# Two groups of a layer's matmuls moved up between the steps of a retention chain

## The chip, the core and the metric

One core of one Trainium2 chip runs the whole program in one launch. The metric is device time in microseconds. The kernel before takes 770.5 us as the median of three runs (770.07 to 770.96). TensorE is called PE here (PEld is its weight load), VectorE is DVE, ScalarE is ACT, GpSimd is POOL, and SP issues the DMAs.

## The reference

Three stages follow each other. Retention (linear attention with a decay per head) makes x; a gated layer without activation multiplies two products of x; a second layer has a leaky activation with a slope for each channel.

```python
batch, n_heads, seq, head_dim = (4, 8, 576, 64)
scores = scale * np.matmul(q, k.transpose(0, 1, 3, 2))
gamma = 1.0 - 2.0 ** (-5.0 - np.arange(H))
Dmat = np.where(rel >= 0, gamma[:, None, None] ** rel[None, :, :], 0.0)
x = np.matmul(scores * Dmat, v)              # then (2304 tokens, 512)
a = x @ w1; b = x @ w2                       # 512 -> 1024
x = (a * b @ w3) @ w_out                     # 1024 -> 1024 -> 512
h = x @ w_in                                 # 512 -> 2048
g = np.maximum(h, 0.0) + alpha * np.minimum(h, 0.0)
out = g @ w_out2                             # 2048 -> 512
```

## The kernel before

**Retention.** The sequence of a batch b is cut into five pieces c (four of 128 tokens, one of 64), and the pieces are taken one after the other, since each carries a state to the next. For batches 1 to 3 this is a chain of 15 links (`chain`, L721); link i treats piece i = 5(b-1)+c. In `link` (L723) PE issues three things: `scores` of the *next* piece (L406, L395 for the short one; PSUM tile `sc`), `values` of this piece (L448 from the state, L457 from the masked scores; tile `o`) and `moments` of the next piece (L421; tile `st`). Everything that other engines do with these results is put on a list, `later`, and issued when the next link begins (`flush`): DVE multiplies `sc` by the mask (L410, L398), and PE's L457 waits for that product; ACT copies `o` into x (L469); DVE adds `st` to the state (L429), and POOL ages it (L433). The pool of `sc` has two buffers (L675), so the scores of piece i+1 may be written while DVE still reads those of piece i. Eight PSUM banks are in use: one for warm-up matmuls, four for `sc`, two for `o`, one for `st`.

**Work beside the links.** The table `beside` (L759) says which preparations for the next stage are issued after which link: `ready` scales q and k of a coming batch (POOL L383, L385; pair 3 on DVE), `ab_steps` prepares the weights' operands, and `x_steps(n)` issues the next n of nine steps that make x's operands of a token pair of blocks p (`x_operands`, L628). A step holds an ACT cast (L637), a DVE subtraction for the low half (L641) and sometimes a DVE difference (L645), each on 128x768.

**First layer.** Its products run in 24 groups of seven (`AbGroup`, L815: p1, p5, p6, p2, p7, p3, p4; a Strassen-like scheme with seven products for eight). A product is six matmuls of 128x384 (L807). The group has three PSUM banks b1, b2, b3; ACT copies b1 to b2 (L830), and b3, b2, b1 to SBUF (L834, L838, L842); DVE makes the two factors from them and multiplies (L847, L852, L859, L860). A finished group is written to DRAM (`spill`). The first three groups begin with a dummy matmul (L827). The groups stand in `ab_order` (L938), n = 0 is weight chunk 0 with p = 0, n = 1 chunk 1 with p = 0, then chunks 0 and 1 with p = 1 and p = 2, then chunk 2 (n = 6 to 8) and so on. Preparations that go beside group n are in `todo`, filled by `at(n, "a" | "b" | "c", ...)` (L950). From n about 5 on this holds the pieces of the folded weights too (`ws_tick`), whose third step is a copy on ACT (L128) of what DVE made (L122).

**Order.** PE, ACT and SP run in the order of the code in the whole kernel; DVE and POOL do so until the end of retention (`ordered`, L690 to L783). After that a list scheduler orders DVE's instructions.

Of the kernel before, what the change touches and what calls it, by code (L numbers as in the profile page):

```python
# [7 lines left out]
F32 = mybir.dt.float32  # L8
# [152 lines left out]
def retention_moe_kernel(ctx: ExitStack, tc, qk, kv, w_out1, w3t, w12, w_in, w_out2, alpha, c_row, c_pair, out):  # L161
# [49 lines left out]
    def kib(flat, at, n):  # L211
        return flat[:, 256 * at:256 * at + n]
# [149 lines left out]
    class Retention:  # L362
# [24 lines left out]
        def scores(self, c):  # L387
            b, n = self.b, self.n
            sc = self.psum["sc"].tile([P, 2, 512], F32, tag="sc", name=f"sc{b}_{c}")
# [278 lines left out]
    def some_of(steps, n):  # L668
        for _ in range(min(n, len(steps))):
            steps.pop(0)()  # L670


    first = ExitStack()
# [76 lines left out]
    def x_steps(n):  # L750
        return lambda: some_of(make, n)

    def to_xr():
# [10 lines left out]
        3: [ready(rs[2], 2), ready(rs[2], 3, nc.vector), x_steps(1)],  # L764
        4: [lambda: load_batch(3), ab_steps(1, "f1"), x_steps(1)],
        5: [x_steps(1), ab_steps(1, "s1")],
        6: [ready(rs[3], 0), x_steps(2)],
        7: [ready(rs[3], 1), x_steps(1), ab_steps(1, "h0")],
        8: [ready(rs[3], 2), ready(rs[3], 3, nc.vector), ab_steps(1, "l0")],
        9: [x_steps(2), ab_steps(1, "h1")],  # L770
        10: [to_xr, lambda: make.extend(ab_operands(1)), ab_steps(1, "l1 h2"), x_steps(1)],
        11: [ab_steps(1, "l2"), x_steps(1)],
        12: [x_steps(1)],
        13: [x_steps(1)],
        14: [x_steps(2)],
    }
    for i in range(-1, len(chain)):
        link(i)()
        for run in beside.get(i, ()):
            run()  # L780
    flush()
    flush()
    ordered.close()  # L783
# [9 lines left out]

    class Group:


        def __init__(self, p, j, n):
            self.p, self.j, self.n = p, j, n
            self.b1, self.b2, self.b3 = (bank((3 * n + m) % 8, f"h{n}_{m}")[:, :W] for m in range(3))

        def product(self, ps, a, b, fresh=True):
            a, b = self.operand(self.j, a), xop[self.p, b]
            n = 0
            for k in range(2):
                ks = slice(k * P, (k + 1) * P)
                for x, y in ((0, 0), (0, 1), (1, 0)):
                    nc.tensor.matmul(ps, a[:, x, ks], b[:, y, k], start=(fresh and n == 0), stop=(n == 5),  # L807
                                     skip_group_check=True)
                    n += 1

    abd = [scratch.tile([P, C1, 2, W], F32, tag=f"ab{p}", name=f"abd{p}") for p in range(NP)]
    fives = [kib(xs, 0, 2 * W)[:, W * m:W * m + W] for m in range(2)]
    pairs_of = [kib(xs, 3 + 3 * m, 2 * W).rearrange("p (t n) -> p t n", t=2) for m in range(3)]

    class AbGroup(Group):  # L815


        operand = staticmethod(ab_operand)

        def __init__(self, p, j, n):  # L820
            super().__init__(p, j, n)
            self.p5s, self.f = fives[n % 2], pairs_of[n % 3]

        def p1(self):
            if self.n < 3:

                nc.tensor.matmul(self.b2, self.operand(self.j, "A11")[:, 0, 0:P], xop[self.p, "B11"][:, 0, 0],  # L827
                                 start=True, stop=True)
            self.product(self.b1, "A11", "B11")
            nc.scalar.copy(self.b2, self.b1)  # L830

        def p5(self):
            self.product(self.b3, "S1", "T1")
            nc.scalar.copy(self.p5s, self.b3)  # L834

        def p6(self):
            self.product(self.b2, "S2", "T2", False)
            nc.scalar.copy(self.f[:, 1], self.b2)  # L838

        def p2(self):  # L840
            self.product(self.b1, "A12", "B21", False)
            nc.scalar.copy(self.f[:, 0], self.b1)  # L842

        def p7(self):
            self.product(self.b2, "S3", "T3", False)
            with soon():
                nc.vector.tensor_tensor(out=self.p5s, in0=self.b2, in1=self.p5s, op=ALU.add)  # L847

        def p4(self):
            self.product(self.b2, "A22", "T4", False)  # L850
            with soon():
                nc.vector.tensor_tensor(out=self.f[:, 0], in0=self.b2, in1=self.f[:, 0], op=ALU.mult)  # L852
            later.append(self.spill)

        def p3(self):
            self.product(self.b3, "S4", "B22", False)
            u = self.f[:, 1]
            with soon():
# [833 lines left out]
```

## Time and profile before

| what | value |
|---|---|
| median of three runs | 770.5 us (770.07 to 770.96) |
| the profiled execution: its own time | 770.14 us |
| its span in the trace | 768.4 us |
| PE busy | 746.7 us (97%) |
| DVE busy | 640.2 us (83%) |
| ACT busy | 428.4 us (56%) |
| POOL busy | 30.2 us (4%) |
| mean granted TensorE clock | 0.991 of full speed |
| last link ends, first layer begins | 88.23 us |

The profile is of one execution, whose own time lies 1.7 us above its span. Busy time of PE counts matmuls by modelled ends, so overlapping ones and those at half the clock count in full; PEld, the weight loads, keeps closer to the pace at which matmuls can be issued. "Idle before" in square brackets behind a row is the engine's idle time just before it, and the arrow names what ended it.

### The profile page before, as it was taken

Reading aid. Unit: us, or ns where it says so; the run is one execution under the profiler, and the core shown is the slowest. Engines: PE = TensorE matmul, PEld = TensorE weight load, DVE = VectorE, ACT = ScalarE, POOL = GpSimd, SP = SyncE. Lnnn points to the kernel's source line nnn. Section 1 sums busy time; section 2 is a strip of 40 time slices with the busy share of each in tenths; the row PEclk is TensorE's granted clock in tenths of the full one; section 3 lists DMA queues with packets and bytes.
Section 4 is the critical chain, followed back from the end, with each engine's and each line's share of the span. In section 5 each row is a group of like instructions: output and inputs, shape, how many; then the busy total and the mean of one; then the engine's idle time right before and its main releaser. Section 6 shows DMA issues by size and latency. Waiting matters only on the chain.

```text
span 768.4 us, 13325 instructions
## 1 busy us (share of the span) xinstructions
PE 746.7 (97%) x4979; PEld 698.3 (91%) x4979; DVE 640.2 (83%) x1061; ACT 428.4 (56%) x754; POOL 30.2 (4%) x35
## 2 busy tenths in 40 slices
PE   8887899999999999999999999999999999999998
PEld 4676899999999988999999999999999888888887
DVE  4899987999799869999997879979877777877884
ACT  3565466666476546666765557556545444444442
POOL 1345000000000000000000000000000000000000
PEclk9899999999999999999999999999999999999999
DMA  9963135676547986587764997666999754434430
GB/s 337 387 249 148 58 123 174 223 242 220 204 170 248 370 315 219 199 308 258 285 225 158 323 369 273 238 208 230 323 351 404 219 158 131 130 120 142 132 122 28
DMA packets 106848, 173.25 MB, mean 225 GB/s; under 512 B 8096, under 2 KB 73888, under 8 KB 106784
## 3 DMA queue, kind: packets, MB, share of 16 engines
q1 hardware_dynamic: 106784, 172.40, 64.7%
q8 instruction: 39, 0.64, 0.3%
q14 instruction: 25, 0.20, 0.1%
HBM read 112.34 MB, written 60.03 MB: 224 GB/s over the span
## 4 chain that ended last, share of the span: by engine, by line
PE 80%; DVE 11%; DMA 5%; issue 2%; ACT 1%; SPq 1%; DVEq 0%; ACTq 0%
PE h L807 37%; PE o L1403 15%; PE y L1219 13%; PE o L1405 8%; PE pw L1059 6%; DMA xs<-in_kv_dram 2%; DMA raw<-in_w_dram 1%; DMA heads_r<-in_kv_dram 1%; DVE wa L641 1%; DVE heads_l L410 1%; PE o L457 1%; DVE xs L645 1%; DVE wa L568 0%; DMA xs<-in_w3t_dram 0%; PE st L421 0%
## 5 line engine op out<-in xcount | busy, mean ns | idle before, releaser
L1219 PE MATMUL y<-yab,wa 128*128 128x384 f32 x576 | 100.2, 334 | 0.0
L1219 PEld LDWEIGHTS y<-yab,wa 128*128 128x128 f32 x576 | 99.8, 188 | 0.3 <-DVE yab L1041 0.2
L1384 DVE TENSOR_TENSOR cells<-cells,cells 128x1024 fp32r<-128x1024 f32 x63 | 76.3, 1220 | 23.3 <-ACT cells L1378 23.3
L1403 PE MATMUL o<-wa,cells 128*128 128x512 f32 x288 | 76.6, 393 | 0.0
L1378 ACT CAST cells<-cells 128x1024 fp32r<-128x1024 f32 x63 | 64.9, 1054 | 5.8 <-DVE cells L1371 5.1
L1403 PEld LDWEIGHTS o<-wa,cells 128*128 128x128 f32 x288 | 51.4, 189 | 8.5
L807 PE MATMUL h<-xB,wa 128*128 128x384 f32 x288 | 58.0, 335 | 0.1
L1403 PE MATMUL o<-wop,cells 128*128 128x512 f32 x216 | 56.9, 392 | 0.0
L807 PE MATMUL h<-xl,wa 128*128 128x384 f32 x288 | 56.2, 336 | 0.6 <-ACT h L830 0.6
L807 PE MATMUL h<-xT,wa 128*128 128x384 f32 x288 | 56.5, 334 | 0.0
L807 PEld LDWEIGHTS h<-xl,wa 128*128 128x128 f32 x288 | 50.2, 188 | 1.9 <-ACT h L830 1.9
L807 PE MATMUL h<-wa 128*128 128x384 f32 x264 | 51.4, 335 | 0.0
L807 PEld LDWEIGHTS h<-xB,wa 128*128 128x128 f32 x288 | 50.5, 188 | 0.6 <-DVE xB L641 0.6
L807 PEld LDWEIGHTS h<-xT,wa 128*128 128x128 f32 x288 | 50.5, 188 | 0.0
L807 PE MATMUL h<-xr,wa 128*128 128x384 f32 x240 | 47.0, 335 | 1.3 <-ACT h L830 0.7
L1403 PEld LDWEIGHTS o<-wop,cells 128*128 128x128 f32 x216 | 39.4, 188 | 7.7
L807 PEld LDWEIGHTS h<-wa 128*128 128x128 f32 x264 | 46.2, 188 | 0.2 <-ACT h L830 0.2
L1405 PEld LDWEIGHTS o<-wa,cells 128*128 128x128 f32 x288 | 41.8, 190 | 3.5
L1405 PE MATMUL o<-wa,cells 128*128 128x256 f32 x288 | 44.5, 282 | 0.0
L807 PEld LDWEIGHTS h<-xr,wa 128*128 128x128 f32 x240 | 41.9, 188 | 1.9 <-ACT h L830 1.0
L1275 DVE SCALAR_TENSOR_TENSOR g<-h,al,g 128x384 f32<-128x384 f32 x48 | 29.1, 612 | 12.1 <-ACT g L1273 10.1
L122 DVE CUSTOM_DVE_ANT_0 a<-a,b 128x1024 uint16<-128x1024 uint16 x56 | 38.3, 685 | 0.5
(238 smaller groups left out, 1535.1 us busy)
## 6 DMA issues: line engine op xcount, KB each, us to landing
gd<-g SPq DMA_DIRECT2D x96, 192.0 KB, 4.5
cells<-gd SPq DMA_DIRECT2D x36, 512.0 KB, 6.0
abd<-xs SPq DMA_DIRECT2D x24, 384.0 KB, 3.2
yf<-abd SPq DMA_DIRECT2D x24, 384.0 KB, 6.2
rawi<-in_w_in_dram SPq DMA_DIRECT2D x16, 512.0 KB, 6.0
wod<-wo2u SPq DMA_DIRECT2D x28, 256.0 KB, 2.6
wa<-wod SPq DMA_DIRECT2D x12, 512.0 KB, 7.0
wod<-xs SPq DMA_DIRECT2D x21, 256.0 KB, 3.1
```

Of the source, the lines that this page charges most:

```text
L122: nc.vector.tensor_tensor(out=a.bitcast(I32), in0=a.bitcast(I32), in1=b, op=ALU.add)
L410: later.append(lambda: nc.vector.tensor_tensor(out=rt, in0=sc[:, :, 0:n * CH].rearrange("p h (n i) -> p h n i", n=n), in1=mask[:, :, self.ps],
L457: nc.tensor.matmul(o[pp, p % 2, m // 2, 0:w], vj, rj, start=(c == 0 and m < 2), stop=True, skip_group_check=True)
L641: nc.vector.tensor_tensor(out=t[:, 1], in0=src[op], in1=_f32(t[:, 0]), op=ALU.subtract)
L807: nc.tensor.matmul(ps, a[:, x, ks], b[:, y, k], start=(fresh and n == 0), stop=(n == 5), skip_group_check=True)
L1059: nc.tensor.matmul(acc[i], a[:, ic], bb, start=(k == 0 and n == 0), stop=(k == C1 - 1 and n == 2))
L1219: nc.tensor.matmul(ys[o], wpc[c][a][:, oc], yab[u][:, bb, c % 2], start=(c == 0 and i == 0), stop=(c == C1 - 1 and i == 2))
L1275: nc.vector.scalar_tensor_tensor(out=g, in0=ps, scalar=sal[:, c], in1=g, op0=ALU.mult, op1=ALU.max)
L1378: nc.scalar.copy(h.bitcast(F32R), self.q[name])
L1384: nc.vector.tensor_tensor(out=l.bitcast(F32R), in0=q[name], in1=h, op=ALU.subtract)
L1403: nc.tensor.matmul(ps, h[:, k], w[k], start=(fresh and k == 0), stop=(k == C1 - 1), skip_group_check=True)
L1405: nc.tensor.matmul(ps[:, 256:], l[:, k], w[k][:, 0:256], start=False, stop=(k == C1 - 1), skip_group_check=True)
```

## The change

The groups n = 0 and n = 1 leave the loop of the layer and are issued inside the chain, a product at a time: one after link 7 has begun, two in each of links 8 to 13 and one in link 14 (`FILLS`). The first product of a link stands ahead of its `scores`, the second behind its `moments`, and what DVE and ACT do with the second one's result goes on `later`. Three PSUM banks are needed for this; they come from the warm-up bank and from the second buffer of `sc`, so from batch 2 on (link 4's `scores`) `sc` has one buffer. The two groups keep their SBUF results in the space of x's block pair 0. The table of x's operands is dealt out anew: block pair 0's nine steps now stand in links 2, 5, 6, 7 and 8 (before: 2 to 7 and 9), block pair 1's first seven in links 10 to 14 (before six), and the rest, with block pair 2's and weight chunk 2's, beside groups 2 to 6 (before: 0 to 6). The class `Group` and `AbGroup` moved up in the file; their unchanged lines are left out here.

```diff
-        return flat[:, 256 * at:256 * at + n]
+        return flat[:, int(256 * at):int(256 * at) + n]
...
         def scores(self, c):
             b, n = self.b, self.n
-            sc = self.psum["sc"].tile([P, 2, 512], F32, tag="sc", name=f"sc{b}_{c}")
+            self.psum["sc"].reverse()
+            sc = (self.psum["sc"][0] if b < 2 else self.psum["late"]).tile([P, 2, 512], F32, tag="sc", name=f"sc{b}_{c}")
...
-        def __init__(self, p, j, n):
+        def __init__(self, p, j, n, banks=None):
             self.p, self.j, self.n = p, j, n
-            self.b1, self.b2, self.b3 = (bank((3 * n + m) % 8, f"h{n}_{m}")[:, :W] for m in range(3))
+            banks = banks or [bank((3 * n + m) % 8, f"h{n}_{m}") for m in range(3)]
+            self.b1, self.b2, self.b3 = (x[:, :W] for x in banks)
+            self.then = lambda run: run()
...
+    EARLY = 2
+    early_of = [(kib(xs, a, W), kib(xs, f, 2 * W).rearrange("p (t n) -> p t n", t=2))
+                for a, f in ((4, 9), (5.5, 0))]
...
-            self.p5s, self.f = fives[n % 2], pairs_of[n % 3]
+            self.p5s, self.f = (fives[n % 2], pairs_of[n % 3]) if n >= EARLY else early_of[n]
...
-            if self.n < 3:
+            if self.n == 0 or EARLY <= self.n < EARLY + 3:
...
             self.product(self.b1, "A11", "B11")
-            nc.scalar.copy(self.b2, self.b1)
+            self.then(lambda: nc.scalar.copy(self.b2, self.b1))
...
-    warm = pool(first, "ps_warm", space=PSUM).tile([P, 512], F32, name="warm")
-    psum0 = {"sc": pool(first, "ps_sc", bufs=2, space=PSUM, reuse_waits="tile"),
+    psum0 = {"late": pool(first, "ps_sc", space=PSUM, reuse_waits="tile"),
...
+    early = ExitStack()
+    warm = pool(early, "ps_warm", space=PSUM).tile([P, 512], F32, name="warm")
+    psum0["sc"] = [psum0["late"], pool(early, "ps_sc1", space=PSUM, reuse_waits="tile")]
...
+    FILLS, fill = {7: 1, 8: 2, 9: 2, 10: 2, 11: 2, 12: 2, 13: 2, 14: 1}, []
+
+    def early_groups():
+        pe = pool(first, "ps_early", space=PSUM, reuse_waits="tile")
+        banks = [pe.tile([P, 512], F32, tag=f"e{m}", name=f"e{m}") for m in range(3)]
+        groups = [AbGroup(0, c, c, banks) for c in range(EARLY)]
+        return [(g, step) for g in groups for step in (g.p1, g.p5, g.p6, g.p2, g.p7, g.p3, g.p4)]
+
     def link(i):
         def run():
             flush()
             nxt = chain[i + 1] if i + 1 < len(chain) else None
+            if i == min(FILLS):
+                early.close()
+                fill.extend(early_groups())
+            n = FILLS.get(i, 0)
+            if n:
+                g, step = fill.pop(0)
+                step()
             if nxt:
                 rs[nxt[0]].scores(nxt[1])
...
                 rs[nxt[0]].moments(nxt[1])
+            if n == 2:
+                g, step = fill.pop(0)
+                g.then = later.append
+                step()
+                g.then = lambda run: run()
...
-        3: [ready(rs[2], 2), ready(rs[2], 3, nc.vector), x_steps(1)],
+        3: [ready(rs[2], 2), ready(rs[2], 3, nc.vector)],
...
-        6: [ready(rs[3], 0), x_steps(2)],
+        6: [ready(rs[3], 0), x_steps(2), ab_steps(1, "s1")],
...
+    abu.load(6)
     ordered.close()
...
-    at(0, "a", x_steps(1))
...
-    at(1, "c", x_steps(2), ab_steps(2, "f0"))
...
+    at(2, "a", x_steps(2), make_p2)
...
+    at(2, "c", x_steps(1), ab_steps(2, "f0"))
+    at(3, "a", x_steps(1), ab_steps(2, "s0 f1"))
+    at(3, "b", x_steps(2))
...
     for n, (c, p) in enumerate(ab_order):
+        if n < EARLY:
+            continue
```

The instructions as they stand in the built programs show what this makes of the queues. First PE in links 7 and 8, before (`sc2_3` are the scores of batch 2's piece 3, `o` the values, `st` the moments):

```order
L406 MATMUL sc2_3_792<-heads_r_103 128x128 x8
L448 MATMUL o2_2_801<-heads_r_103,heads_l_99 64x128 x8
L457 MATMUL o2_2_801<-heads_l_99,heads_r_103 64x128 x8
L421 MATMUL st2_3_818<-heads_r_103 64x64 x8
L395 MATMUL sc2_4_837<-heads_r_103 64x64 x8
L448 MATMUL o2_3_846<-heads_r_103,heads_l_99 64x128 x8
L457 MATMUL o2_3_846<-heads_l_99,heads_r_103 64x128 x8
```

The same two links now (`e0` to `e2` are the three banks of the early groups; the lines of the file have shifted: L406 is L407 now, L807 is L689):

```order
L712 MATMUL e1_801<-wa_63 128x384
L689 MATMUL e0_800<-wa_63 128x384 x6
L407 MATMUL sc2_3_811<-heads_r_103 128x128 x8
L449 MATMUL o2_2_820<-heads_r_103,heads_l_99 64x128 x8
L458 MATMUL o2_2_820<-heads_l_99,heads_r_103 64x128 x8
L422 MATMUL st2_3_837<-heads_r_103 64x64 x8
L689 MATMUL e2_802<-wa_63 128x384 x6
L396 MATMUL sc2_4_866<-heads_r_103 64x64 x8
L449 MATMUL o2_3_875<-heads_r_103,heads_l_99 64x128 x8
L458 MATMUL o2_3_875<-heads_l_99,heads_r_103 64x128 x8
L689 MATMUL e1_801<-wa_63 128x384 x6
```

Three products of six matmuls stand between the links' own matmuls, and `sc2_3` goes into the tile from which DVE still has to take `sc2_2`.

Second, DVE in links 10 and 11, before (L410 is the mask's product, L427 and L429 the state, L568 a weight operand):

```order
L410 TENSOR_TENSOR heads_l_99<-sc3_0_878,heads_l_99 128x1024
L427 COPY heads_l_99<-st3_0_904 128x256
L568 SCALAR_TENSOR_TENSOR wa_63<-xs_95,wa_63 128x512
L645 TENSOR_TENSOR xs_95<-xs_95 128x768
L410 TENSOR_TENSOR heads_l_99<-sc3_1_921,heads_l_99 128x1024
L429 TENSOR_TENSOR heads_l_99<-heads_l_99,st3_1_939 128x256
```

The same now (L734 to L755 take the results of the early group from `e1` and `e2`):

```order
L411 TENSOR_TENSOR heads_l_99<-sc3_0_924,heads_l_99 128x1024
L428 COPY heads_l_99<-st3_0_950 128x256
L734 TENSOR_TENSOR xs_95<-e1_801,xs_95 128x384
L754 TENSOR_TENSOR xs_95<-e2_802,xs_95 128x384
L755 TENSOR_TENSOR xs_95<-xs_95 128x384
L569 SCALAR_TENSOR_TENSOR wa_63<-xs_95,wa_63 128x512
L646 TENSOR_TENSOR xs_95<-xs_95 128x768
L642 TENSOR_TENSOR xr_1016<-xs_95,xr_1016 128x768
L646 TENSOR_TENSOR xs_95<-xs_95 128x768
L411 TENSOR_TENSOR heads_l_99<-sc3_1_979,heads_l_99 128x1024
L430 TENSOR_TENSOR heads_l_99<-heads_l_99,st3_1_997 128x256
```

Between two mask products there were three instructions, and there are eight.

Third, ACT in group 6 of the layer, which is the same before and now but for names (`h6_1` is bank b2 of group 6; its copy waits in line behind L128):

```order
L128 CAST xs_95<-xs_95 128x512
L98 ACTIVATE xs_95<-xs_95 128x512
L99 ACTIVATE xs_95<-xs_95 128x512
L564 CAST ux_91<-xs_95 128x512
L564 CAST ux_91<-a5_1312 128x256
L715 COPY h6_1_1522<-h6_0_1521 128x384
```

What feeds this L128 on DVE is the fourth instruction of the first folded weight piece, and it stands 51 rows behind the last mask product of retention (rows 118 to 168 of DVE); the same rows hold what is left of x's operands for p = 1, all of p = 2 and chunk 2's operands.

## Rows read from the trace of the kernel before

**Rows 1.** The page's first part: busy time, share and instructions of each engine.

```profile
PE 746.7 (97%) x4979; PEld 698.3 (91%) x4979; DVE 640.2 (83%) x1061; ACT 428.4 (56%) x754; POOL 30.2 (4%) x35
```

**Rows 2.** Busy time by stretch; links 7 to 14 are 60.66 to 88.23.

```profile
core 0: us, PE busy (x) PEld busy (x) DVE busy (x) ACT busy (x) POOL busy (x), PEclk, DMA share, GB/s
...
49.00:52.40 3.40, 1.89 (x35) 1.41 (x34) 3.40 (x6) 3.21 (x5) 1.18 (x2) 1.00 0.24 34
52.40:55.80 3.40, 3.40 (x48) 3.17 (x48) 2.67 (x4) 1.18 (x3) 1.03 (x1) 0.50 0.82 285
...
60.66:66.10 5.44, 2.75 (x52) 2.31 (x50) 5.44 (x6) 3.48 (x6) 3.08 (x3) 1.00 0.75 291
66.10:69.50 3.40, 3.40 (x56) 2.96 (x54) 3.40 (x6) 2.19 (x5) 3.40 (x4) 0.50 0.03 7
69.50:88.23 18.73, 15.23 (x336) 13.10 (x332) 18.43 (x26) 8.31 (x15) 3.75 (x5) 1.00 0.07 21
88.23:99.96 11.73, 11.73 (x75) 11.73 (x68) 8.89 (x12) 7.21 (x15) 0.00 (x0) 1.00 0.20 60
```

**Rows 3.** Timeline of links 7 and 8: start, us, engine, line, tiles [idle before].

```profile
60.66 1.16 PE L406 MATMUL sc<-heads_r 64*128 64x128 f32 x16
...
60.97 2.03 DVE L641 TENSOR_TENSOR wa<-xs,wa 128x768 fp32r<-128x768 f32 x1
...
63.92 1.21 DVE L410 TENSOR_TENSOR heads_l<-sc,heads_l 128x1024 f32<-128x1024 f32 x1
...
65.18 1.16 PE L457 MATMUL o<-heads_l,heads_r 128*64 128x128 f32 x16 [2.06 <-DVE heads_l L410]
...
68.76 1.77 DVE L568 SCALAR_TENSOR_TENSOR wa<-a,wa 128x512 fp32r<-128x512 f32 x1
```

**Rows 4.** Timeline of link 12 and the beginning of link 13's DVE work.

```profile
80.22 0.94 PE L406 MATMUL sc<-heads_l 64*128 64x128 f32 x12
80.28 0.94 DVE L641 TENSOR_TENSOR xr<-xs,xr 128x768 fp32r<-128x768 f32 x1
...
81.15 0.95 DVE L645 TENSOR_TENSOR xs<-xs 128x768 f32<-128x768 f32 x1
...
82.02 1.21 DVE L410 TENSOR_TENSOR heads_l<-sc,heads_l 128x1024 f32<-128x1024 f32 x1
83.16 0.40 DVE L429 TENSOR_TENSOR heads_l<-heads_l,st 128x256 f32<-128x256 f32 x1
...
83.48 1.21 DVE L410 TENSOR_TENSOR heads_l<-sc,heads_l 128x1024 f32<-128x1024 f32 x1
```

**Rows 5.** Timeline of PE as the layer begins: dummies and two successive products' middles.

```profile
88.23 0.44 PE L827 MATMUL h<-wa 128*128 128x384 f32 x1
...
94.93 1.20 PE L807 MATMUL h<-wa 128*128 128x384 f32 x6
...
95.97 1.20 PE L807 MATMUL h<-wa,ux 128*128 128x384 f32 x6
...
99.96 0.19 PEld L827 LDWEIGHTS h<-xr,wa 128*128 128x128 f32 x1
```

**Rows 6.** Timeline of DVE beside group 5 of the layer.

```profile
125.69 0.42 DVE L118 TENSOR_SCALAR xs<-xs 128x512 uint32<-128x512 uint32 x1
126.02 0.68 DVE L122 CUSTOM_DVE_ANT_0 a<-a,b 128x1024 uint16<-128x1024 uint16 x1
...
127.23 0.55 DVE L859 TENSOR_TENSOR xs<-h,xs 128x384 f32<-128x384 f32 x1
127.69 0.68 DVE L122 CUSTOM_DVE_ANT_0 xs<-xs 128x1024 uint16<-128x1024 uint16 x1
```

**Rows 7.** Timeline of ACT in group 6: the folded piece's copy and the group's first.

```profile
130.62 0.62 ACT L128 CAST xs<-xs 128x512 fp32r<-128x512 f32 x1
...
133.09 0.49 ACT L830 COPY h<-h 128x384 f32<-128x384 f32 x1
```

**Rows 8.** Waits after 88 us: engine, line, waited for: us in total, times, longest.

```profile
PEld h L807 <- ACT h L830: 3.1, 7, 1.0
```

More of the change, by code (lines that the diff above doesn't have):

```diff
@@ L670, in some_of, with product @@
             steps.pop(0)()
+    class Group:
+        def __init__(self, p, j, n, banks=None):
+            self.p, self.j, self.n = p, j, n
+            banks = banks or [bank((3 * n + m) % 8, f"h{n}_{m}") for m in range(3)]
+            self.b1, self.b2, self.b3 = (x[:, :W] for x in banks)
+            self.then = lambda run: run()
+        def product(self, ps, a, b, fresh=True):
+            a, b = self.operand(self.j, a), xop[self.p, b]
+            n = 0
+            for k in range(2):
+                ks = slice(k * P, (k + 1) * P)
+                for x, y in ((0, 0), (0, 1), (1, 0)):
+                    nc.tensor.matmul(ps, a[:, x, ks], b[:, y, k], start=(fresh and n == 0), stop=(n == 5),
+                                     skip_group_check=True)
+                    n += 1
@@ new lines, in retention_moe_kernel, with __init__, p1, p5 @@
+    abd = [scratch.tile([P, C1, 2, W], F32, tag=f"ab{p}", name=f"abd{p}") for p in range(NP)]
+    EARLY = 2
+    early_of = [(kib(xs, a, W), kib(xs, f, 2 * W).rearrange("p (t n) -> p t n", t=2))
+                for a, f in ((4, 9), (5.5, 0))]
+    fives = [kib(xs, 0, 2 * W)[:, W * m:W * m + W] for m in range(2)]
+    pairs_of = [kib(xs, 3 + 3 * m, 2 * W).rearrange("p (t n) -> p t n", t=2) for m in range(3)]
+    class AbGroup(Group):
+        operand = staticmethod(ab_operand)
+        def __init__(self, p, j, n, banks=None):
+            super().__init__(p, j, n, banks)
+            self.p5s, self.f = (fives[n % 2], pairs_of[n % 3]) if n >= EARLY else early_of[n]
+        def p1(self):
+            if self.n == 0 or EARLY <= self.n < EARLY + 3:
+                nc.tensor.matmul(self.b2, self.operand(self.j, "A11")[:, 0, 0:P], xop[self.p, "B11"][:, 0, 0],
+                                 start=True, stop=True)
+            self.product(self.b1, "A11", "B11")
+            self.then(lambda: nc.scalar.copy(self.b2, self.b1))
+        def p5(self):
+            self.product(self.b3, "S1", "T1")
+            self.then(lambda: nc.scalar.copy(self.p5s, self.b3))
+        def p6(self):
+            self.product(self.b2, "S2", "T2", False)
+            self.then(lambda: nc.scalar.copy(self.f[:, 1], self.b2))
+        def p2(self):
+            self.product(self.b1, "A12", "B21", False)
+            self.then(lambda: nc.scalar.copy(self.f[:, 0], self.b1))
+        def p7(self):
+            self.product(self.b2, "S3", "T3", False)
+            def out():
+                with soon():
+                    nc.vector.tensor_tensor(out=self.p5s, in0=self.b2, in1=self.p5s, op=ALU.add)
+            self.then(out)
+        def p4(self):
+            self.product(self.b2, "A22", "T4", False)
+            def out():
+                with soon():
+                    nc.vector.tensor_tensor(out=self.f[:, 0], in0=self.b2, in1=self.f[:, 0], op=ALU.mult)
+                later.append(self.spill)
+            self.then(out)
+        def p3(self):
+            self.product(self.b3, "S4", "B22", False)
+            u = self.f[:, 1]
+            def out():
+                with soon():
+                    nc.vector.tensor_tensor(out=u, in0=self.b3, in1=u, op=ALU.add)
+                    nc.vector.tensor_tensor(out=u, in0=u, in1=self.p5s, op=ALU.mult)
+            self.then(out)
+        def spill(self):
+            nc.sync.dma_start(out=abd[self.p][:, self.j], in_=self.f)
@@ L780, in retention_moe_kernel @@
             run()
+    assert not fill
     flush()
     flush()
+    abu.load(6)
     ordered.close()
@@ L811, in retention_moe_kernel @@
[L811 to L821, printed above, removed]
-            self.p5s, self.f = fives[n % 2], pairs_of[n % 3]
-        def p1(self):
-            if self.n < 3:
-                nc.tensor.matmul(self.b2, self.operand(self.j, "A11")[:, 0, 0:P], xop[self.p, "B11"][:, 0, 0],
-                                 start=True, stop=True)
-            self.product(self.b1, "A11", "B11")
-            nc.scalar.copy(self.b2, self.b1)
[L832 to L858, printed above, removed]
-                nc.vector.tensor_tensor(out=u, in0=self.b3, in1=u, op=ALU.add)
-                nc.vector.tensor_tensor(out=u, in0=u, in1=self.p5s, op=ALU.mult)
-        def spill(self):
-            nc.sync.dma_start(out=abd[self.p][:, self.j], in_=self.f)
```

47 lines of the change are left out of this document (15 added, 32 removed).

## The prediction

> **What bounds the kernel now.** I read the page's busy times first, then the busy time by stretch, then the timeline of the links and of the layer that follows. On the page PE is busy for 97% of the span [rows 1], so only time in which PE can issue nothing is to be had. The reader finds such time in the stretches of the links [rows 2]: from 60.66 to 88.23, links 7 to 14, the weight loads fill 2.31 + 2.96 + 13.10 = 18.4 us of 27.6, and in the same stretches DVE is busy for 5.44 of 5.44, 3.40 of 3.40 and 18.43 of 18.73 us. So the links are DVE's, and PE waits for it: L457 stood 2.06 us until the mask's product had come [rows 3]. In the layer it is the other way: from 88.23 to 99.96 PE is busy for all 11.73 us, DVE for 8.89 [rows 2].
>
> The change carries PE work from where PE is the bound to where DVE is, and DVE work along with it. What counts is how much longer the links get, and whether DVE comes late into the layer.
>
> **What leaves the layer.** Two products in a row begin at 94.93 and 95.97, so one costs 1.04 us [rows 5]. From the first dummy at 88.23 to that of group 2 at 99.96 lie 11 of the two groups' 14 products; three more follow among those of group 2. Without the change both groups are done at 99.96 + 3 x 1.04 = 103.1 if nothing else ran. The dummies go from three (n = 0, 1, 2) to four (0, 2, 3, 4); at 0.17 us each (11.73 less 11 x 1.04 = 0.29 for two) that costs 0.3 in the layer. The layer can therefore begin with group 2 as late as 102.8 and nothing is lost; each microsecond that the chain ends before that is a gain.
>
> **How long the chain gets.** First its beginning. Links 3 and 4 lose one step's L641 and one L645 that now come in link 7 or later; start to start these are 81.15 - 80.28 = 0.87 and 82.02 - 81.15 = 0.87 [rows 4]. DVE has little pause there (3.40 of 3.40, then 2.67 of 3.40 [rows 2]), so link 7 begins some 1.7 us earlier, at about 58.9.
>
> Then PE's own work in links 7 to 14: 18.4 us by the weight loads (an upper value, since 2.96 of it ran at half the clock) and 14 products with one dummy, 14.7 us. Were PE never to wait, the chain would end at 58.9 + 33.1 = 92.0, a gain of 10.8 us. That is the bound on the good side.
>
> PE will wait in the links where DVE has more to do than PE. The order now gives DVE's work link by link, and the steps have prices: mask 1.14, state 0.32, L641 and L645 0.87 each [rows 4], a group's eviction 0.46, an L118-like or a 256-column operation 0.33, one of the L122 or L568 kind 0.6 (two of them from 126.02 to 127.23) [rows 6].
> - Link 7: mask, state, 2 x L641, L645 make 4.1. POOL scales q beside it, and an L641 that fell on it took 2.03 us instead of 0.94 [rows 3, 4], so 1.1 more: 5.2. PE has about 18.4 / 8 = 2.3 of its own, one product and a dummy: 3.5. Excess 1.7.
> - Link 8: mask, state, pair 3's scaling (one of 0.6, one of 0.33), 2 x L641, an L568 (0.6), four differences of 256 columns (1.3) make 6.1, and 1.1 for POOL again, since L568 took 1.77 us there [rows 3]: 7.2. PE 2.3 + 2.1 = 4.4. Excess 2.8.
> - Link 10: mask, state, three evictions, L568, three of the 0.87 kind make 6.1 against 4.4. Excess 1.7.
> - Link 9 (0.3), 11 (3.8), 12 (3.2), 13 (3.7) lie under PE's 4.4; link 14 waits for a short mask alone.
>
> Together 6.2 us of waiting. The second buffer of `sc` would have let the next scores run during it; with one buffer they stand behind the mask's product, so I don't count on a link's excess being caught up in the next. The chain ends at 92.0 + 6.2 = 98.2. It could be 1.5 less (the 18.4 is too high by up to half of 2.96, were the clock full) or 3 more (if in links 7, 8 and 10 DVE also has to wait for the scores behind its mask, 0.94 each [rows 4]). I take 98.2: gain 102.8 - 98.2 = 4.6, from 6.1 to 1.6.
>
> **What the layer gives back.** The evictions of the early groups are off DVE in the layer (8 x 0.46 = 3.7 us, most of it), but 14.7 us of PE time under which DVE worked are gone too. In the order, 51 rows of DVE (52 instructions) stand between the last mask's product and the L122 that the folded weights' first copy (L128) needs: 14 of the 0.87 kind, 15 evictions or products of 0.46, 13 of 0.33, 10 of 0.6 make 12.2 + 6.9 + 4.3 + 6.0 = 29.4 us. DVE starts them when link 14 begins, 1.6 us before the chain's end (one product and some 0.6 of values), at 96.6; without any pause it is through at 126.0. In 88.23 to 99.96 it paused for 11.73 - 8.89 = 2.84 us [rows 2], for results of ACT and PE; 2 to 5 us of this kind in the whole stretch make 128 to 131.
>
> ACT is in order, and group 6's copy L830 stands behind that L128: begun 133.09 against 130.62, and as long as an eviction of its own (0.49), so 3.0 us from one to the other's end [rows 7]. It would be done at 131 to 134. PE wants it for the third product of group 6, that is after 27 products of groups 2 to 5, two of group 6 and three dummies: 98.2 + 29 x 1.04 + 0.5 = 128.9. PE waits for 2 to 5 us. If DVE never paused, 126.0 + 3.0 = 129.0: no wait; if the waits in groups 3 to 5 come on top, up to 6. I take 3.2. Before, all waits of this kind in the trace after 88 us come to 3.1 us in seven, the longest 1.0 [rows 8]; one of these is replaced, so 2.2 net, from 0 to 5.
>
> **The clock.** The granted clock fell to half, the 1.2 GHz level, twice: in 52.40 to 55.80, after a stretch in which the weight loads filled 1.41 of 3.40 us, and in 66.10 to 69.50, after one with 2.31 of 5.44 [rows 2]. The wait ahead of 52.40 shrinks with the steps that leave links 3 and 4. But link 7's product now ends before the mask is through, and PE stands for about its excess and what link 6 left; and PE stands again in group 6. Both are as long as the 2.06 us ahead of the second fall. A stretch of 3.4 us at half the clock loses 1.7 us of PE work where PE is the longer side, and less where it waits for DVE anyway, as in links 7 and 8. I take 1.6 for both, from 0 to 3.4; the stretches that go are inside the traced times already, and what they gave is in the 1.7 us by which link 7 comes early.
>
> The Trainium skill (TensorE: Matmul & The Clock Gate, section "Part 1: The HAM clock gate") states that the low clock is the default, that activity lifts it, and that the place of the switch shifts from run to run. By that rule a slow stretch needn't fall where this trace puts it, and could cover a link with two products as well as one with a wait. This run has one pattern and cannot show the others; by it some runs would have a third stretch, and the sum would be up to 1.7 higher there, +0.9.
>
> **The sum.** -4.6 + 2.2 + 1.6 = -0.8 us. The profiled execution's own time is 770.14 (span 768.4 and 1.7 around it), so 769.3; it lies 0.36 under the median of the runs, and I forecast 769.7 for a median.
>
> **Rivals.**
> - DVE is not late in the layer. For it: DVE paused in the traced layer (2.84 of 11.73 us), and a list scheduler orders it there. Against: 29.4 us of work in front of one copy, and the time has shrunk from 40 to 31 us. Then -4.6 with at most 0.3 of clock: about 766.2.
> - The clock stays low over several stretches in links 7 to 11, because PE stands in 7, 8 and 10 and each slow stretch makes products take 2.1 us in place of 1.04. Three stretches with PE the longer side cost 3 x 1.7 = 5.1 in place of 1.6: -4.6 + 2.2 + 5.1 = +2.7, so 773.2. From two and a half such stretches on it decides, and the kernel is slower. For it: two falls in this trace, each after such a wait. Against: 69.50 to 88.23 runs at the full clock with 18.73 - 15.23 = 3.5 us of PE idle in it [rows 2], and the products fill PE.
> - The change doesn't do what it says: the products take the place of nothing, since with one `sc` buffer mask and scores alternate and each link grows by its products. The chain then ends at 88.23 + 14.7 = 102.9, nothing is won, and the late DVE costs up to 2.2: 770.5 to 772.7. Against: PE has 9.2 us free there by its loads.
>
> **Chances.** Forecast 0.52, the late clock rival 0.16, DVE not late 0.22, nothing won 0.10. A change of 0.2%, 1.5 us, is about what a measurement of this kernel can tell from none; so faster is under 769.0 and slower over 772.0. The forecast's own range is 768.4 to 772.0, and it gives 0.13 to faster, 0.37 to same, 0.02 to slower. DVE not late is faster; the clock rival slower; of nothing won 0.05 each to same and slower. Faster 0.35, same 0.42, slower 0.23. The range for 8 in 10 goes halfway into the first two rivals: 766.6 to 772.9.
>
> **What would show it.** In the profile after, the first L712 of group 2 stands at 97 to 99; before it PE waits for DVE ahead of the scores in links 7, 8 and 10 and hardly in 9 and 11 to 13. DVE has no pause from 60 to 96. In group 6 PE waits 2 to 5 us for ACT, ACT for DVE at L128. If the layer begins after 101, the link sums are wrong; if group 6 doesn't wait, the 29.4 us are; if the clock row shows no half level after 58, that term is. Past 300 us everything should stand as before, shifted as a block.

## The result, and the profile after

The changed kernel takes 776.51 us (median; 775.45 to 779.29), the one before 770.73 in the same runs (769.70 to 771.81). The ratio is 1.0077, with a 95% interval of 1.0058 to 1.0096: slower by some 6 us, where 769.7 was forecast in a range of 766.6 to 772.9. The profiled execution took 776.87 us, its span 775.1.

The page's first part, which answers to [rows 1]: PE's busy time has grown by 3.4 us and the span by 6.7, and DVE has 3 us less.

```profile
PE 750.1 (97%) x4980; PEld 699.7 (90%) x4980; DVE 637.2 (82%) x1061; ACT 428.5 (55%) x754; POOL 29.6 (4%) x35
```

The busy times link by link say most. First link 11 and the sum of such a table for before, cut at the beginnings of links 7 to 14 (60.66 to 88.23):

```profile
76.96:80.22 3.26, 3.25 (x68) 2.82 (x65) 3.26 (x5) 0.59 (x3) 1.00 (x1) 1.00 0.03 5
...
sum 27.57, PE 21.38 PEld 18.37 DVE 27.27 ACT 13.98 POOL 10.23; mean PE 3.05 PEld 2.62 DVE 3.90 ACT 2.00 POOL 1.46
```

And after, where the same links are 60.66 to 106.30 (columns as in [rows 2]):

```profile
core 0: us, PE busy (x) PEld busy (x) DVE busy (x) ACT busy (x) POOL busy (x), PEclk, DMA share, GB/s
60.66:70.83 10.17, 6.07 (x76) 5.13 (x72) 9.03 (x11) 5.90 (x11) 4.21 (x4) 0.83 0.65 259
70.83:75.20 4.37, 4.37 (x64) 3.77 (x61) 3.19 (x6) 3.26 (x8) 2.06 (x2) 1.00 0.01 4
75.20:83.15 7.95, 5.97 (x77) 5.32 (x76) 4.79 (x9) 3.77 (x8) 0.61 (x1) 0.79 0.00 0
83.15:88.27 5.12, 5.12 (x63) 4.68 (x62) 4.08 (x7) 0.59 (x1) 0.00 (x0) 1.00 0.01 3
88.27:94.50 6.23, 5.44 (x77) 4.76 (x77) 6.00 (x9) 2.59 (x5) 0.61 (x1) 1.00 0.17 66
94.50:100.00 5.50, 5.50 (x78) 4.89 (x77) 4.05 (x5) 2.28 (x4) 1.26 (x1) 1.00 0.00 0
100.00:106.30 6.30, 6.30 (x101) 5.39 (x100) 4.30 (x7) 2.53 (x4) 0.00 (x0) 1.00 0.01 3
sum 45.64, PE 38.78 PEld 33.95 DVE 35.45 ACT 20.92 POOL 8.76; mean PE 5.54 PEld 4.85 DVE 5.06 ACT 2.99 POOL 1.25
```

The reader is to see three things. The links are 18.07 us longer, and the 14 products that came in are worth 14.7 in the layer. PE is busy for all of links 8, 10, 12 and the last stretch. And DVE, which was busy for 27.27 of 27.57 us, now is for 35.45 of 45.64: it is no longer what the links wait for, save in links 7, 9 and 11. The prediction's own sign, a layer that begins after 101, came true: its first dummy stands at 106.19 (the table is cut at the first product behind it).

Link 7, in the timeline of after (answers to [rows 3]):

```profile
56.00 0.59 ACT L470 COPY xs<-o 128x512 f32<-128x512 f32 x1 [1.38 <-PE o L458]
...
60.07 0.91 ACT L376 ACTIVATE heads_l<-heads_l,al 128x256 f32<-128x256 f32 x2 [3.48 <-DMA heads_l<-in_kv_dram]
...
60.88 1.55 ACT L638 CAST wa<-xs 128x768 fp32r<-128x768 f32 x2
...
61.73 0.96 DVE L642 TENSOR_TENSOR wa<-xs,wa 128x768 fp32r<-128x768 f32 x1 [3.11 <-ACT wa L638]
...
62.61 0.95 DVE L646 TENSOR_TENSOR xs<-xs 128x768 f32<-128x768 f32 x1
...
63.47 0.42 DVE L113 TENSOR_SCALAR a<-a 128x512 f32<-128x512 f32 x1
63.93 0.43 DVE L116 TENSOR_SCALAR a<-a 128x512 uint32<-128x512 uint32 x1
...
64.39 0.69 DVE L122 CUSTOM_DVE_ANT_0 a<-a,b 128x1024 uint16<-128x1024 uint16 x1
65.00 1.22 DVE L411 TENSOR_TENSOR heads_l<-sc,heads_l 128x1024 f32<-128x1024 f32 x1
...
66.27 2.08 PE L407 MATMUL sc<-heads_r 64*128 64x128 f32 x16 [4.10 <-DVE heads_l L411]
```

The chain is read backwards: PE's scores wait for the mask (L411), with one buffer; the mask stands on DVE behind x's L642 and L646 and behind the step `s1` (L113, L116, L122), which the change moved here from link 5; L642 waits for ACT's casts (L638); and the casts stand on ACT behind the scaling of batch 3 (L376), which waited 3.48 us for its DMA. In the timeline of before, ACT came to the same scaling later, behind a copy at 57.14 that stands at 56.00 in after, and waited for nothing:

```profile
57.14 0.58 ACT L469 COPY xs<-o 128x512 f32<-128x512 f32 x1 [2.85 <-PE o L457]
...
57.63 0.91 ACT L376 ACTIVATE heads_l<-heads_l,al 128x256 f32<-128x256 f32 x2
```

The transfer came later as well: SP issued batch 3's first one at 52.77, in before at 50.89.

In link 9 the profile names no releaser for PE's wait, but the mask of the short piece ends at 78.38, just ahead of the scores:

```profile
77.96 0.42 DVE L399 TENSOR_TENSOR heads_l<-sc,heads_l 128x256 f32<-128x256 f32 x1
...
78.48 0.94 PE L407 MATMUL sc<-heads_l 64*128 64x128 f32 x12 [1.98 <-issue]
```

The layer, in the timeline (answers to [rows 7]), the waits after 88 us (answers to [rows 8]) and two stretches of the clock:

```profile
136.31 0.68 DVE L122 CUSTOM_DVE_ANT_0 xs<-xs 128x1024 uint16<-128x1024 uint16 x1
...
137.08 0.62 ACT L128 CAST xs<-xs 128x512 fp32r<-128x512 f32 x1 [2.85 <-DVE xs L122]
...
139.56 0.46 ACT L715 COPY h<-h 128x384 f32<-128x384 f32 x1
...
140.07 1.04 PEld L689 LDWEIGHTS h<-wa 128*128 128x128 f32 x6 [2.61 <-ACT h L715]
```

```profile
PEld h L689 <- ACT h L715: 5.2, 7, 2.6
```

```profile
79.52:82.94 3.42, 3.42 (x55) 3.13 (x53) 1.65 (x2) 1.93 (x4) 0.57 (x1) 0.50 0.00 0
...
140.96:144.38 3.42, 3.42 (x13) 3.42 (x12) 3.42 (x9) 0.96 (x2) 0.00 (x0) 0.50 0.66 252
```

PE's weight loads wait 2.61 us in group 6, by the chain that the prediction named, and then PE runs for 3.42 us, from 140.96, at the 1.2 GHz level.

### The profile page after: what moved, and what is told of

Read it like the earlier page. It is cut to its first block, busy times and chain, and to the rows that moved or that the text cites. A ratio compares the mean times of both kernels' runs of the same rounds, so it can differ in the third digit from the quotient of the medians.

```text
span 775.1 us, 13326 instructions
## 1 busy us (share of the span) xinstructions
PE 750.1 (97%) x4980; PEld 699.7 (90%) x4980; DVE 637.2 (82%) x1061; ACT 428.5 (55%) x754; POOL 29.6 (4%) x35
## 4 chain that ended last, share of the span: by engine, by line
PE 67%; DVE 16%; DMA 10%; issue 3%; ACT 2%; SPq 1%; DVEq 0%; ACTq 0%
PE h L689 29%; PE o L1443 15%; PE y L1259 8%; PE o L1445 8%; DMA wod<-xs 3%; PE o L458 2%; PE e L689 2%; PE sc L407 2%; DMA wv<-wud 2%; DVE a L120 2%; DVE a L122 1%; DMA raww<-in_w3t_dram 1%; DVE a L113 1%; DMA heads_r<-in_kv_dram 1%; DMA gd<-g 1%
## 5 line engine op out<-in xcount | busy, mean ns | idle before, releaser
L689 PE MATMUL h<-xB,wa 128*128 128x384 f32 x288 | 57.9, 335 | 0.1
L689 PE MATMUL h<-xl,wa 128*128 128x384 f32 x288 | 56.8, 339 | 1.0 <-ACT h L715 1.0
L689 PE MATMUL h<-xT,wa 128*128 128x384 f32 x288 | 56.5, 334 | 0.0
L689 PEld LDWEIGHTS h<-xl,wa 128*128 128x128 f32 x288 | 50.7, 190 | 2.6 <-ACT h L715 2.6
L689 PEld LDWEIGHTS h<-xB,wa 128*128 128x128 f32 x288 | 50.5, 188 | 0.6 <-DVE xB L642 0.6
L689 PEld LDWEIGHTS h<-xT,wa 128*128 128x128 f32 x288 | 50.5, 188 | 0.0
L689 PE MATMUL h<-xr,wa 128*128 128x384 f32 x240 | 46.6, 335 | 0.6 <-DVE xs L734 0.6
L689 PEld LDWEIGHTS h<-xr,wa 128*128 128x128 f32 x240 | 42.0, 188 | 0.9 <-DVE xs L734 0.9
L689 PE MATMUL h<-wa 128*128 128x384 f32 x198 | 39.9, 342 | 2.3 <-ACT h L715 2.3
L122 DVE CUSTOM_DVE_ANT_0 a<-a,b 128x1024 uint16<-128x1024 uint16 x56 | 38.2, 684 | 0.5
L689 PEld LDWEIGHTS h<-wa 128*128 128x128 f32 x198 | 35.6, 192 | 2.6 <-ACT h L715 2.6
```

The lines of the kernel that those rows point to most:

```text
L122: nc.vector.tensor_tensor(out=a.bitcast(I32), in0=a.bitcast(I32), in1=b, op=ALU.add)
```

## The experiments

All times are medians beside the kernel before on the same chip: 770.73 us beside the changed kernel, and 769.3, 769.7 and 769.6 in three later sittings with the other kernels. Since before itself differs by 1.4 us between sittings, kernels of different sittings are better compared by their ratios, which have 95% intervals. In the table, "x first" writes x's steps ahead of the scaling of batch 3, and "late pieces" starts the folded weights' pieces one group later.

| kernel | us | ratio to before |
|---|---|---|
| changed kernel | 776.51 | 1.0077 (1.0058 to 1.0096) |
| new table alone | 775.80 | 1.0078 (1.0053 to 1.0103) |
| table, one buffer | 778.47 | 1.0122 (1.0098 to 1.0147) |
| changed, x's steps first | 772.77 | 1.0035 (1.0020 to 1.0050) |
| changed, one group in the links | 777.69 | 1.0096 (1.0068 to 1.0124) |
| table, x's steps first | 773.99 | 1.0048 (1.0030 to 1.0067) |
| changed, old links 3 to 7 | 775.79 | 1.0062 (1.0039 to 1.0085) |
| changed, x first, late pieces | 769.74 | 0.9994 (0.9975 to 1.0013) |
| the same with old links 3 to 7 | 770.84 | 1.0022 (0.9999 to 1.0046) |
| before, bare links 9 to 13 | 776.32 | 1.0090 (1.0070 to 1.0110) |
| before, late pieces | 770.31 | 1.0011 (0.9998 to 1.0024) |
| before, one buffer | 773.36 | 1.0052 (1.0033 to 1.0070) |
| table, x first, late pieces | 772.59 | 1.0045 (1.0028 to 1.0062) |

**The new table of x's operands alone**

```diff
-    EARLY = 2
+    EARLY = 0
-    FILLS, fill = {7: 1, 8: 2, 9: 2, 10: 2, 11: 2, 12: 2, 13: 2, 14: 1}, []
+    FILLS, fill = {}, []
```
(and two buffers for the scores everywhere)

> The changed kernel with the new table of x's operands, but no group in the links (all 24 stand in the layer) and two score buffers throughout. Handover theory (one score buffer makes masks and scores alternate): as before, 770 to 771.5. ACT-line theory (POOL's and ACT's scaling of the next batch waits for a DMA and stands ahead of x's casts in ACT's line, so DVE and then PE stand): 2 to 3 us slower than before, 773, since the line is the same here. Dose theory (a link of PE has less room than 18.4/8 us said, so products lengthen it): as before.

Measured 775.80. No product has left the layer, and the loss is there, larger than any of the three theories had it. I had priced the moving of x's steps by DVE alone. The timeline of this kernel has the same chain as after (it is of the slowest of the six executions, 779.78, so it shows the chain and not its share):

```profile
59.34 0.91 ACT L376 ACTIVATE heads_l<-heads_l,al 128x256 f32<-128x256 f32 x2 [3.30 <-DMA heads_l<-in_kv_dram]
...
60.15 1.55 ACT L638 CAST wa<-xs 128x768 fp32r<-128x768 f32 x2
...
60.99 0.96 DVE L642 TENSOR_TENSOR wa<-xs,wa 128x768 fp32r<-128x768 f32 x1 [2.76 <-ACT wa L638]
```

**The same with one buffer for the scores from batch 2 on**

```diff
-            sc = self.psum["sc"][0].tile(...)
+            sc = (self.psum["sc"][0] if b < 2 else self.psum["late"]).tile(...)
```

> As the run with the new table alone, but with one score buffer from batch 2 on; no group in the links. Handover theory: 4 us or more slower than the run with two buffers, near 775, PE waiting for the mask ahead of the scores in most links. ACT-line and dose theories: as the run with two buffers within 1 us.

Measured 778.47, 2.7 more than the table alone: between what the theories had, and the intervals overlap slightly. From here the changed kernel differs by the products only, and takes 2.0 us less by the medians, 3.5 by the ratios: the products do win something, after the rest has lost more. By the ratios the table costs 6.0 us, the one buffer 3.4, and the products give back 3.5.

**x's steps ahead of the scaling**

```diff
-        6: [ready(rs[3], 0), x_steps(2), ab_steps(1, "s1")],
+        6: [x_steps(2), ready(rs[3], 0), ab_steps(1, "s1")],
```
(and so in links 7 and 8)

> The changed kernel with x's steps issued ahead of the scaling of batch 3 in links 6, 7 and 8; nothing else differs. ACT-line theory: 3 us faster than the changed kernel, about 773.5, and PE's wait of 4.1 us ahead of the scores in link 7 shrinks to about 1. Handover and dose theories: within 1 us of the changed kernel, 776 to 777.

Measured 772.77: 3.7 us back by the medians, 3.2 by the ratios, and the interval lies wholly under that of the changed kernel. The timeline shows the casts now done before the wait:

```profile
54.65 1.56 ACT L638 CAST wa<-xs 128x768 fp32r<-128x768 f32 x2
...
57.73 0.91 ACT L376 ACTIVATE heads_l<-heads_l,al 128x256 f32<-128x256 f32 x2 [1.52 <-DMA heads_l<-in_kv_dram]
...
62.88 1.53 PE L407 MATMUL sc<-heads_r 64*128 64x128 f32 x14 [2.56 <-DVE heads_l L411]
```

Link 7 still waits 2.56 us, where the theory had about 1: in link 6 now stands the step of chunk 1 (`s1`) that stood in link 5, and DVE does it ahead of the mask. With `s1` back in link 5, and x's steps of links 3 to 7 too, the wait is 1.91 and 1.90 us (two kernels below). The layer is untouched by this edit, and PE's weight loads stand there as long as in after (2.62 us at 134.57).

**One group in the links instead of two**

```diff
-    EARLY = 2
+    EARLY = 1
-    FILLS, fill = {7: 1, 8: 2, 9: 2, 10: 2, 11: 2, 12: 2, 13: 2, 14: 1}, []
+    FILLS, fill = {8: 1, 9: 1, 10: 1, 11: 1, 12: 1, 13: 1, 14: 1}, []
```

> The changed kernel with only group 0 in the links, one product in each of links 8 to 14; group 1 is in the layer. Dose theory: half of the loss, 773 to 774. Handover theory: nearly the whole loss, 775 to 776, since the one score buffer is there as before. ACT-line theory: 775, since the line in link 6 is the same.

Measured 777.69, more than any of the three theories had: half the products cost no less, so a link's load of products is not what loses. The scaling waits 4.01 us for its DMA in this profile, and PE 6.06 us in link 7. Links 11 and 12 of this kernel, with one product each, in the table by stretch:

```profile
89.84:94.26 4.42, 4.42 (x70) 3.81 (x70) 3.96 (x6) 2.02 (x4) 1.38 (x2) 1.00 0.00 0
94.26:98.69 4.43, 4.43 (x71) 3.82 (x70) 3.75 (x5) 1.32 (x2) 0.23 (x1) 1.00 0.01 4
```

**The table alone, x's steps first**

> The new table of x's operands alone (no product leaves the layer, two buffers for the scores everywhere), with x's steps written ahead of the scaling of batch 3 in links 6 to 8. With the scaling first the same table took 775.8 (+6). Theory of ACT's line: the loss is made where x's casts stand on ACT behind a scaling that waits for its DMA (3.30 us at 59.34 in the table's run), so with the casts first the table costs little: 770 to 771.5. Rival, the table costs because DVE's work has left links 3 and 4, where it had cover, and comes in links 5 to 8 and in the layer, where it has none: 774 to 776 again. A third: half of it is made in the layer (the table's run lost 2.4 us between the chain's last product and group 7), then 772.5 to 773.5.

Measured 773.99: at the edge of the rival's 774 to 776 and above the third theory's 772.5 to 773.5. It is only 1.8 us under the table alone, with intervals that overlap. So ACT's line is not the whole of the table's price. In group 6 of the layer PE's weight loads still wait 1.96 us here.

**The changed kernel with links 3 to 7 as before**

```diff
-        3: [ready(rs[2], 2), ready(rs[2], 3, nc.vector)],
+        3: [ready(rs[2], 2), ready(rs[2], 3, nc.vector), x_steps(1)],
...
-        6: [ready(rs[3], 0), x_steps(2), ab_steps(1, "s1")],
+        6: [ready(rs[3], 0), x_steps(2)],
```

(and links 4, 5, 7 and 8 to match)

> The changed kernel with the products in the links, but with x's steps in links 3 to 7 as they were before (one each in 3, 4 and 5, two in 6, one in 7) and the last two in link 8; the scaling stays ahead of x's steps. Theory of ACT's line: in link 6 x's casts have less to catch up and the scaling's DMA has landed by then, so link 7's wait of 4.1 us falls to about 1 and the time to 772 to 773, as with x's steps first. Rival, the one buffer of scores and the products make links 7 to 10 long by themselves: 775.5 to 777, link 7 as long as in the changed kernel.

Measured 775.79, as the rival had it, though link 7's wait fell from 4.10 to 1.91 us, most of the way to the theory's 1:

```profile
64.36 1.23 PE L407 MATMUL sc<-heads_r 64*128 64x128 f32 x16 [1.91 <-DVE heads_l L411]
```

In the two traces half of this kernel's distance to x's steps first lies ahead of the layer, and the other half past 344 us, where the two kernels have the same code. The traced execution of x's steps first took 770.70, 2.1 us under its median, so part of that distance is spread between executions. The medians are 3.0 us apart (2.1 by the ratios), and no run here explains that.

**x's steps first, and the folded weights' pieces one group later**

```diff
-        m = 14 + WS * n // 10
+        m = 17 + WS * n // 10
```

> The changed kernel with x's steps first (772.8) and the pieces of the folded weights started one group later throughout (their first step at group 5's last place and not group 4's). Theory: ACT's copy for group 6 waits behind the first piece's copy, which waits for a late DVE (PE stood 2.30 us there, then a stretch of 3.4 us at half the clock); with the piece a group later that wait goes and 2.3 + 1.7 - 1.0 come back: 769.5 to 770.5. Rival, DVE's backlog after the links is the cause and the wait goes to another place (an eviction in group 5 or 6, or group 7 behind the piece): 772 to 773.5.

Measured 769.74: 3.0 us back from 772.77 (3.2 by the ratios), and no difference from before. In the timeline of ACT, group 6's copy no longer has the piece's copy ahead of it (131.21; the L128 comes at 138.53, a group later), and what PE waits behind the piece's copy in group 7 is small:

```profile
131.21 0.48 ACT L715 COPY h<-h 128x384 f32<-128x384 f32 x1
...
138.53 0.62 ACT L128 CAST xs<-xs 128x512 fp32r<-128x512 f32 x1 [3.03 <-DVE xs L122]
...
140.16 0.48 ACT L715 COPY h<-h 128x384 f32<-128x384 f32 x1
...
140.70 1.36 PEld L689 LDWEIGHTS h<-xr,wa 128*128 128x128 f32 x8 [0.83 <-ACT h L715]
```

The layer has no stretch at half the clock in this profile. Links 11 and 12, with two products each:

```profile
85.99:91.48 5.49, 5.49 (x77) 4.88 (x77) 5.27 (x9) 3.08 (x6) 1.53 (x2) 1.00 0.19 75
91.48:96.96 5.48, 5.48 (x78) 4.87 (x77) 2.81 (x3) 2.73 (x5) 0.34 (x1) 1.00 0.00 0
```

**All three together** (products in the links with x's steps of links 3 to 7 as before, x's steps first, late pieces)

> All three together: products in the links, x's steps in links 3 to 7 as before and the last two in 8, ahead of the scaling, and the folded weights' pieces one group later. If the losses are separate (ACT's line in link 6, the late DVE at group 6) the two products' gain shows: 767.5 to 769.5, less than before's 769.3 to 770.7. Rival, the links with products are as long as PE's own work makes them (5.5 us for a link with two), so that nothing is won beside before: 770 to 772.

Measured 770.84, by the rival: nothing is won beside before (the interval is 0.9999 to 1.0046).

**What a link costs PE by itself**

```diff
-        9: [x_steps(2), ab_steps(1, "h1")],
-        10: [to_xr, lambda: make.extend(ab_operands(1)), ab_steps(1, "l1 h2"), x_steps(1)],
-        11: [ab_steps(1, "l2"), x_steps(1)],
-        12: [x_steps(1)],
-        13: [x_steps(1)],
-        14: [x_steps(2)],
+        14: [x_steps(2), ab_steps(1, "h1"), to_xr, lambda: make.extend(ab_operands(1)),
+             ab_steps(1, "l1 h2"), ab_steps(1, "l2"), x_steps(6)],
```

> The kernel before, with all that DVE and ACT do beside the retention in links 9 to 13 (x's steps and the splits of chunk 1) moved to link 14; nothing is left out. It measures what a link costs PE by itself. The prediction took 2.3 us a link, from the busy time of the weight loads, and the other 1.1 us of a link's 3.3 to 3.4 us (start to start of the scores, links 8 to 10 of before) as waiting for DVE. By that, links 9 to 13 take 2.3 to 2.6 us with DVE freed. Theory now: a link is 3.1 to 3.4 us of PE's own (its small matmuls don't follow one another at the pace of their weight loads), since a link took 3.3 with no product, 4.42 with one and 5.49 with two. By that, they take 3.1 to 3.4 us here too. The time of the whole is of no matter: the moved steps stand ahead of the layer, so 774 to 782.

Links 10 to 12 of this kernel in the table by stretch:

```profile
72.21:74.79 2.58, 2.58 (x52) 2.39 (x48) 1.73 (x3) 0.34 (x1) 0.62 (x1) 1.00 0.00 0
74.79:77.97 3.18, 3.18 (x68) 2.82 (x64) 1.65 (x2) 0.59 (x3) 0.61 (x1) 1.00 0.02 5
77.97:81.15 3.18, 3.18 (x68) 2.82 (x65) 1.65 (x2) 0.65 (x3) 0.62 (x1) 1.00 0.03 5
```

The whole takes 776.32, in the range expected. DVE is half empty in the links, and a full link still takes 3.18 us, with PE busy for all of it. Link 10, with fewer matmuls (52 for 68), takes 2.58, and PE is busy for all of that too. So the theory of PE's own time is right. With one product a link is 4.42, with two 5.49: the links grow by the products' whole time and more, 1.24 for one and 2.31 for two, where a product in a row with others costs 1.04 [rows 5]. The 2.82 of weight loads is less than the link, and so was not the measure of PE's work, for which the text ahead of the prediction took it. The Trainium skill (Perfetto Trace Analysis, section "Identifying the Most-Contended Engine") advises to judge TensorE's headroom by its share of peak FLOPs (MFU) or by the busy share of LDWEIGHTS, and not by matmul busy time. Here the measurement says otherwise: by the loads a link has 11% to spare, by matmul busy time none, and none is what products found.

**Late pieces in the kernel before**

> The kernel before, with only the pieces of the folded weights one group later. If PE's wait of 1.04 us in group 6 of before is all that this can give back: 768.7 to 769.7, against before's 769.7. If the same edit's 3 us in the changed kernel came from something that before has too: 766.5 to 767.5. If later waits (1.28 to 1.48 us at 215 us in the kernels with late pieces, 0.79 in before) eat it: 769.7 to 770.5.

Measured 770.31, in the third range by its median, and no difference by its interval. The 1.04 us are group 7's, at 141.93; in group 6 PE's weight loads wait only 0.20 us in before. A wait of the size that the edit cures is a thing of the changed kernel.

**One buffer in the kernel before**

> The kernel before, with one buffer for the scores from batch 2 on. With the new table of x's operands that cost 2.7 us (775.8 to 778.5). Theory of the handover: the scores of a link then wait until the mask's product of the link before is through, in eight links or so, 0.3 to 0.6 us each: 772 to 774. Rival, PE works its links through at its own pace of 3.3 us, and the wait only shows where DVE is late: 769.7 to 771.

Measured 773.36: the second buffer is worth 3.8 us by itself. The scores' waits of links 7, 11 and 12 in the timeline:

```profile
65.13 2.08 PE L407 MATMUL sc<-heads_r 64*128 64x128 f32 x16 [3.40 <-DVE heads_l L411]
...
80.97 0.94 PE L407 MATMUL sc<-heads_l 64*128 64x128 f32 x12 [0.70 <-DVE heads_l L411]
...
85.53 0.71 PE L407 MATMUL sc<-heads_l 64*128 64x128 f32 x8 [1.31 <-DVE heads_l L411]
```

**The table alone, x's steps first, late pieces**

> The new table alone with x's steps first (774.0) and the folded weights' pieces one group later. If the table's loss in the layer is the same wait of group 6 (PE stood some 1.9 us ahead of group 7 in the table's run), 1.9 less what before has there comes back: 772 to 773. If it is spread over the chain (three stretches at half the clock, 10.24 us, from 63.76), it stays at 773.5 to 774.5. The distance from here to 769.7, which is this with the products and one buffer, is what the products win.

Measured 772.59, in the range for group 6's wait by its median; but by the ratios (1.0045, and 1.0048 without late pieces) the late pieces give back nothing here, so the run doesn't settle it. By the ratios (1.0045 and 0.9994) the products with one buffer are worth 3.9 us beside this kernel.

## Why the prediction was wrong

- **What leaves the layer** held to 1.4 us. The kernel with x's steps first and late pieces has group 2's dummy at 101.94 and begins its last matmul at 765.00, before at 764.52. So a layer that begins at 101.5 would have ended level, and by the kernel with all three at 101.4 (101.21 and 764.38); 102.8 had been worked out.
- **How long the chain gets** is the step that failed. The forecast was 98.2 for its end, and it came at 106.30, 8.1 us later. Taken apart: it began at 60.66, not 58.9, but that profile was 1.9 us late already at the scores of link 3 (47.51, before 45.62), ahead of the first moved step; the profiles of the other kernels have them at 45.0 to 47.1. Against that, link 7 came as early as forecast. PE's own work was 38.78 us in place of 33.1, so 5.7 more: 3.0 because the weight loads (18.4) were read as PE's work where PE's busy time is 21.4, and 2.7 because the 14 products and their dummy took 38.78 - 21.38 = 17.4 us among small matmuls, partly at half the clock, in place of 14.7. PE waited 45.64 - 38.78 = 6.9 us, and 6.2 had been forecast. The amount was nearly right by luck, for the reason was not: 4.10 us in link 7 (forecast 1.7), by ACT's line behind a DMA and by `s1`; 1.98 in link 9 and 0.79 in link 11, where a late mask held the scores; and none in links 8 and 10, where 2.8 and 1.7 had been forecast.
- The sentence that the links are DVE's was half a reading. DVE was busy for 18.43 of 18.73 us there [rows 2], but so was PE for 3.25 of 3.26 in link 11: two engines filled the same link, and taking work from the one doesn't free the other. The bare links show it. The prediction counts 9.2 us of free PE in all the links by the loads, where PE's busy time leaves 27.57 - 21.38 = 6.2; the 3.5 us that it gives in a rival for 69.50 to 88.23 are by busy time, and right.
- **The one buffer** was written down as a reason against catching up and given no price. By itself, in the kernel before, it costs 3.8 us.
- **Moving x's steps** was priced by DVE alone. Its other engine, ACT, does the casts in the order of the program, behind a scaling that waits for a DMA. In the changed kernel, writing the casts first gives back 3.7 us (3.2 by the ratios).
- **What the layer gives back** held: ACT's L128 came at 137.08, 6 to 9 us after the 128 to 131 forecast, as the whole was 8.1 late, and PE's weight loads waited 2.61 us (forecast 3.2, from 2 to 5). Waits of this kind after 88 us grew from 3.1 to 5.2 us, so 2.1 net for 2.2. That this came so close was partly luck: the wait of 1.0 that was taken as replaced stood in group 7, and group 6's own was 0.20. The late pieces gave 3.0 us back.
- **The clock** was forecast at 1.6 us, from 0 to 3.4. After's granted clock is at half in 65.87 to 69.28 (there before, too), and newly in 79.52 to 82.94 and 140.96 to 144.38: two stretches, the upper end. The one that before has from 52.40 is gone.
- The rival that nothing is won (770.5 to 772.7) was right that each link grows by its products, but by another mechanism, and it lacked the losses of the table. The rival of the low clock isn't what happened: two new stretches, one in the links. Nor is the one that DVE is not late in the layer, for PE waited for it there.

With 8.1 us put in the chain's place, the forecast would have been 777.8, beside 776.5 measured. What the experiments don't settle is where the table's last 3.5 us go (1.0045, with x first and late pieces). In that kernel's profile the layer begins at 90.09, before at 88.23, and the last matmul begins 2.1 us later than before's, so most of it is made in the chain. It has three stretches of 3.41 us at half the clock in a row from 63.34, where before has one there and one from 52.40. The two other profiles of the table with two buffers have three in a row as well (from 64.44 and 63.76). That they are the cause is argued, not shown.

Two things made ACT wait for batch 3's transfer in after: SP issued it 1.9 us later than in before, as late as the whole profile was, and ACT came to it 1.1 us earlier. The lateness is not needed: in the profiles with one group in the links and with the table and one buffer, which were 0.2 and 0.5 us late at link 3, ACT waited 4.01 and 2.69 us for the same transfer.

## What to carry to other kernels

Before work is put into an engine's gaps, measure the gaps by that engine's busy time (weight loads are a part of it), and measure them link by link: an engine that is full doesn't say that the other one is free. A step that is moved takes a place in the line of every engine that it uses, so look for the wait that it now stands behind on each. A second buffer that is given up to make room has a price of its own, to be weighed before the gain.

## What the runs showed that I had not expected

- Products of 128x384 between the retention's small matmuls cost 1.15 to 1.24 us each, in a row 1.04.
- In the layer, the clock fell to the 1.2 GHz level after each of the three waits of the weight loads of 2.61 to 2.62 us in group 6, and after none of the four of 1.93 to 2.25 in other kernels' profiles. In the links it fell after a shorter one as well (2.27 us ahead of 78.45 in after, the fall at 79.52). The Trainium skill (TensorE: Matmul & The Clock Gate, section "Part 1: The HAM clock gate") says that the place of a switch shifts from run to run. The stretches of the first 80 us do begin at other times in each profile, but these are profiles of different kernels, so no run here shows it by itself.
